# Tying the weight scans to a tile of their own, splitting an exchange in four, and starting running sums with a copy

## The chip, the cores and the metric

The kernel runs on one core of a Trainium2 chip. The metric is the device time in microseconds (us) of one execution. A core has a matrix engine (PE, with its weight loads as PEld), a vector engine (DVE), a scalar engine (ACT), a general engine (POOL) and a sequencer that issues most of the DMAs (SP). Each engine and SP work through a list of instructions in a fixed order; an instruction that has to wait for a semaphore holds up all that stands behind it in the same list.

## What is computed

A transformer block on 2048 tokens of width D = 576: a layer norm that is shifted and scaled by a conditioning vector, linear attention with 32 heads, a residual, a second such norm, and a feed-forward layer of width 4608 with SiLU. Cut to what matters:

```python
mod = (silu(c) @ w_mod)                      # 6 vectors: sa, ca, ga, sb, cb, gb
h = layernorm(x) * (1 + ca) + sa
x = x + ga * attention(h, wqkv, wo)          # phi(q), phi(k), kv = phi(k)^T v, normalised
h = layernorm(x) * (1 + cb) + sb
x = x + gb * (silu(h @ w1) @ w2)             # w1: 576 x 4608, w2: 4608 x 576
```

The kernel takes the feed-forward products in 16-bit halves (a rounded part and a rest). So that nothing overflows, the weights and values are scaled by powers of two, and these powers are found from the weights themselves: a sum of squares over the columns of w1 and over the rows of w2.

## The kernel before

The hidden width of 4608 is cut into 18 groups `g` of 256 columns. Two neighbouring groups share one set of scale factors (`factor`, lines 201 to 203). To find the factors of such a pair, `scans` (line 737) loads 512 columns of `B_w1` and 512 rows of `B_w2` piece by piece (line 759, on SP) and squares each piece on ACT with a running total (line 760). `find_factors` (line 763) then adds the totals on DVE (770, 771), writes them to DRAM (772) and reads them back to all partitions (773), which is the exchange of limits, and goes on with about ten tiny instructions: a reduce (774), a multiply (775), a maximum (776), a power on POOL (777), then a mask, reciprocals and products on DVE (778 to 787).

The work has three stages.

1. *Tiles.* A loop over 16 tiles `t` of 128 tokens projects keys and values (`k_proj`, `v_proj`; line 285 is the matmul), adds up `kv_mm` (712) and, for the first half, projects queries. The tokens of the next four tiles are loaded as a block (`load_block`, 333), normalised, turned by way of DRAM (`turn_block`, 340 to 350) and modulated (`turn`, 255 and 261) on the way. PE follows the order of the text. The order of the other engines is written out by hand in `FIRST` and laid on by `arrange`, as no-wait dependencies from each instruction to the one before it in the list.
2. *Attention output and the first group.* A loop over steps `s`: `q_norm`, `q_transpose`, `attn_out`, the second norm, and the feed-forward of group 0. In its end, and in the first two slots of the third stage, group 1 is worked with products of a Strassen kind, and their order is written out in `ORDERS`.
3. *Groups 2 to 17.* 32 slots, in an order found when the kernel is built by a planner (`Schedule`) with a duration for every step and named rooms that are read and written. Running sums are kept in `accb` and in four rooms `U`, which POOL sets to zero (1791) before `down_add` (1661) adds the first product from PSUM.

The scans and factor arithmetic of the first pair (groups 0 and 1) belong to stage 1, in `find_first`, called at the end of each tile; those of the second pair (groups 2 and 3) belong to stage 2, in `find_second`, called at the start of each step; the later pairs are steps of the planner. The instructions of the first two are `loose`: they are in no hand-written order, and the scheduler puts each where its simulation finds the engine free and the operands there. So a scan may stand in ACT's list a long way ahead of the tile in whose text it is.

Of the kernel before, what the change touches and what calls it, by code (L numbers as in the profile page):

```python
# [24 lines left out]
def kernel(ctx: ExitStack, tc, A_x, A_wqkv, A_wo, B_x, B_w1, B_w2, c, w_mod, out):  # L25
# [117 lines left out]

    def loose(*made):
        free.update(i.ins.name for i in made)

    def arrange(orders, start):
        for engine, text in orders.items():
            traced = [i for i in nc.cur_bb.bb.instructions[start:] if i.engine == getattr(mybir.EngineType, engine)
                      and i.name not in free  # L150
                      and not isinstance(i, (mybir.BassTilePoolBoundary, mybir.InstTileManualSchedule, mybir.InstRegisterMove))]
            before = None
            for part in text.split():
                first, *last = part.split("-")
                for i in traced[int(first) : int(last[0] if last else first) + 1]:
                    if before is not None:
                        no_wait = mybir.DependencyInfo(mybir.DependencyClass.NoSync, mybir.DependencyReason.DATA)
                        tc.add_manual_dep(i, before.name, no_wait, reason="arrange")
                    before = i
# [39 lines left out]
    sets = [const.tile([P, 8], F32, name=f"set{i}") for i in range(2)]  # L199

    def factor(g, name):
        i = ("beta", None, "delta", "gamma", "inv", "kappa", "out", "ratio").index(name)
        return sets[g // 2 % 2][:, i : i + 1]
# [533 lines left out]
    def scans(G_, spots, st, n, width):  # L737

        f0 = 2 * G_ * FW
        made = []  # L740
        for j in range(0, 9, n):
            m = min(n, 9 - j)
            spot = spots[len(made) % len(spots)]
            at_, to = spot[:, : m * FW], st[:, 0, j // n : j // n + 1]
            load = [(at_[64 * h : 64 * h + 64], B_w1[:, f0 + h * FW : f0 + (h + 1) * FW].rearrange("(p j) f -> p j f", j=9)[:, j : j + m])
                    for h in range(2)]
            made.append((load, at_, to, m))
        flat = B_w2[f0 : f0 + 2 * FW, :].rearrange("a b -> (a b)").rearrange("(p n) -> p n", p=P)
        k = 0
        while k < 4 * D:  # L750
            m = min(width, 4 * D - k)
            spot = spots[len(made) % len(spots)]
            to = st[:, 1, k // width : k // width + 1]
# [3 lines left out]
        for load, at_, to, m in made:  # L757
            def fetch_part(load=load, m=m):
                return [nc.sync.dma_start(dst if m is None else dst.rearrange("p (j f) -> p j f", j=m), src) for dst, src in load]
            parts.append((fetch_part, lambda at_=at_, to=to: A.activation(at_, at_, AF.Square, accum_out=to)))  # L760
        return parts

    def find_factors(G_, st, n1, n2, small, every):

        own, q, half = small[:, 0:2], small[:, 2:6], small[:, 6:10]
        s8, before = sets[G_ % 2], sets[(G_ + 1) % 2]
# [47 lines left out]
    first_scans = scans(0, [z], found, 2, D)  # L814
    first_steps = [step for _, step in find_factors(0, found, 5, 4, crowp[:, 12:22], z[:, : 2 * P])]

    def scan_first(n):
        if 0 < n <= len(first_scans):
            loose(first_scans[n - 1][1]())
        if n < len(first_scans):  # L820
            loose(*first_scans[n][0]())

    def find_first(t):

        if t == 2:
            loose(V.memset(crowp[:, 18:22], 0.5))
# [21 lines left out]
    if True:  # L848
        for t in range(NT):
            tb, i = t // 4, t % 4  # L850
            more = tb + 1 < NB
            if i == 0 and more and t > 0:
# [46 lines left out]
            find_first(t)  # L899
# [4 lines left out]
    with tc.manual_schedule(engines={mybir.EngineType.PE}):  # L904
# [64 lines left out]
        for j in range(KC + 1):  # L969
# [12 lines left out]
            if j in (0,):  # L982
                q_proj(next(qs))
    psA.release()
# [279 lines left out]
    slots = [(1, 0), (1, 1)] + [(g, p) for i in range(2, NG, 2) for p in range(2) for g in (i, i + 1)]  # L1264
# [153 lines left out]
    def find_second(s):  # L1418

        if s == 8:  # L1420
            rest = rests["hT"][0]
            spots = [rest[:, 1152 * i : 1152 * i + 1152] for i in range(2)]
# [688 lines left out]
```

## Time and profile before

| | us |
|---|---|
| median of 3 runs | 1131.14 |
| the runs | 1127.79 to 1132.87 |
| the profiled execution | 1126.87 |
| its span (first to last instruction) | 1125.2 |
| PE busy | 1083.8 |
| DVE busy | 899.4 |
| ACT busy | 690.5 |
| POOL busy | 655.8 |

The page gives busy time for each engine; a waits answer says what ended the idle time in front of an instruction; a timeline answer lists an engine's instructions in order of time, with the idle time ahead of each in square brackets and the name of what released it. A windows answer gives the busy time of each engine in a stretch, then the TensorE clock that was granted (1.00 is full) and the load of the DMA engines. Since PE is busy for nearly all of the span, the places where it is not are what counts.

### The profile page before, as it was taken

The numbers are of one execution on the slowest core, as the hardware profiler recorded it, in microseconds if no ns is written. First come the engines' busy times: TensorE is split into PE (matmuls) and PEld (weight loads), VectorE is DVE, ScalarE is ACT, GpSimd is POOL, SyncE is SP. The second block draws the span as 40 slices with busy tenths as digits, with TensorE's granted clock in tenths as the row PEclk, the third lists the DMA queues.
The fourth block names the chain that finished last, engine by engine and source line by source line (L and its number), as shares of the span: only waits on it lengthen the run. The fifth ranks groups of instructions, "written<-read, shape, count | busy, mean of one in ns | idle before, by whom it ended". The sixth has DMA issues, their size and how long they took to land.

```text
span 1125.2 us, 19368 instructions
## 1 busy us (share of the span) xinstructions
PE 1083.8 (96%) x7137; PEld 777.7 (69%) x7137; DVE 899.4 (80%) x1478; ACT 690.5 (61%) x1336; POOL 655.8 (58%) x759
## 2 busy tenths in 40 slices
PE   8799999998999988899999999999999999999998
PEld 7788999898888544566666666666666666666665
DVE  7548865757797989989889889789889789888757
ACT  5633442354655668777677677677677677676654
POOL 3300000254472468958958948848948848957663
PEclk9999999999999999999999999999999999999999
DMA  9494958062224565858666656656567657635522
GB/s 287 123 226 83 163 144 108 9 171 58 77 95 149 202 219 174 284 128 264 200 187 225 207 178 225 203 181 226 199 183 227 202 181 226 209 114 178 172 84 106
DMA packets 120079, 193.53 MB, mean 172 GB/s; under 512 B 43372, under 2 KB 78064, under 8 KB 119984
## 3 DMA queue, kind: packets, MB, share of 16 engines
q1 hardware_dynamic: 119812, 191.99, 58.2%
q8 instruction: 56, 0.92, 0.3%
q14 instruction: 39, 0.32, 0.1%
q10 hardware_dynamic: 172, 0.30, 0.1%
HBM read 176.77 MB, written 15.48 MB: 171 GB/s over the span
## 4 chain that ended last, share of the span: by engine, by line
PE 78%; DMA 9%; DVE 5%; ACT 3%; POOL 2%; issue 1%; SPq 1%; ACTq 0%; DVEq 0%; POOLq 0%
PE up L1566 30%; PE down L1650 29%; PE psK L285 8%; PE big L285 5%; DMA z<-in_B_w_dram 3%; PE small L1080 2%; PE big L1091 1%; DMA acc<-in_A_wqkv_dram 1%; DMA hT<-in_B_w_dram 1%; DMA hT<-hd 1%; DMA xt<-in_A_x_dram 1%; PE kvp L712 1%; PE psK L975 1%; PE small L270 1%; PE big L1005 1%
## 5 line engine op out<-in xcount | busy, mean ns | idle before, releaser
L1566 PE MATMUL up<-hT,w 128*128 128x512 f16 x1264 | 317.9, 381 | 7.9 <-DMA hT<-hd 4.7
L1566 PEld LDWEIGHTS <-w 128*128 128x128 f16 x1492 | 146.5, 98 | 143.2 <-issue 10.6
L1659 DVE SCALAR_TENSOR_TENSOR acc<-acc,set,down 128x576 f32<-128x576 f32 x128 | 103.6, 810 | 31.2 <-PE down L1650 29.7
L1584 ACT ACTIVATE f<-f,set 128x512 f32<-128x512 f32 x102 | 73.4, 720 | 77.4 <-DVE f L1590 67.6
L285 PE MATMUL psK<-w,hT 128*128 128x256 f32 (+1 forms) x638 | 104.3, 300 | 10.4 <-DVE vx L162 5.8
L1604 POOL TENSOR_TENSOR s<-f,f 128x256 f32<-128x256 f32 x66 | 54.0, 818 | 100.9 <-ACT f L1585 98.5
L285 PEld LDWEIGHTS psK<-w,hT 128*128 128x128 f32 x638 | 92.7, 191 | 12.2 <-issue 6.1
L1650 PE MATMUL down<-w,hb 128*128 128x288 f16 x600 | 89.3, 287 | 3.4 <-DVE U L1661 3.4
L1650 PE MATMUL down<-w,hc 128*128 128x288 f16 x600 | 88.9, 286 | 0.0
L1650 PE MATMUL down<-w,hT 128*128 128x288 f16 x480 | 82.8, 286 | 0.4 <-DVE acc L1661 0.4
L1588 DVE TENSOR_TENSOR f<-up,p 128x512 f32<-128x512 f32 x102 | 69.7, 683 | 16.2 <-PE up L1566 10.6
L1650 PEld LDWEIGHTS <-hb 128*128 128x128 f16 x600 | 58.9, 98 | 25.5 <-issue 3.0
L1585 ACT ACTIVATE f<-f,set 128x512 f32<-128x512 f32 x102 | 73.6, 722 | 3.3
L1650 PEld LDWEIGHTS <-hc 128*128 128x128 f16 x600 | 58.7, 98 | 21.5
L238 POOL TENSOR_TENSOR rstd<-ve,neghalf 128x4 f32<-128x4 f32 (+3 forms) x10 | 9.9, 992 | 108.4 <-DVE ve L237 107.6
L1628 POOL TENSOR_TENSOR hc<-s,hc 128x512 f16<-128x512 f32 x50 | 62.7, 1254 | 5.0 <-ACT hc L1624 5.0
L1650 PEld LDWEIGHTS <-hT 128*128 128x128 f16 x480 | 47.0, 98 | 26.6 <-issue 0.8
L1590 DVE TENSOR_TENSOR f<-up,f 128x512 f32<-128x512 f32 x68 | 46.8, 688 | 19.3 <-PE up L1566 18.5
L1601 POOL TENSOR_TENSOR s<-f 128x256 f32<-128x256 f32 x66 | 55.9, 848 | 8.9 <-ACT f L1581 7.1
L285 PE MATMUL big<-w,qT 128*128 128x288 f32 x352 | 54.7, 304 | 4.0 <-DVE qT L162 3.9
L1608 POOL TENSOR_TENSOR f<-f,s 128x256 f32<-128x256 f32 x66 | 50.4, 763 | 12.8 <-DVE hb L1628 9.0
L1606 POOL TENSOR_TENSOR s<-s,f 128x256 f32<-128x256 f32 x66 | 54.8, 830 | 3.0
(378 smaller groups left out, 2698.7 us busy)
## 6 DMA issues: line engine op xcount, KB each, us to landing
hT<-hd SPq DMA_DIRECT2D x101, 640.0 KB, 4.4
hT<-hd SPq DMA_DIRECT2D x65, 512.0 KB, 4.1
hT<-in_B_w_dram SPq DMA_DIRECT2D x16, 576.0 KB, 6.8
hT<-in_B_w_dram SPq DMA_DIRECT2D x32, 256.0 KB, 4.6
raw<-in_B_w_dram SPq DMA_DIRECT2D x9, 576.0 KB, 4.0
v<-in_B_w_dram SPq DMA_DIRECT2D x9, 576.0 KB, 6.2
xt<-in_A_x_dram SPq DMA_DIRECT2D x16, 288.0 KB, 7.1
raw<-in_w_mod_dram SPq DMA_DIRECT2D x8, 576.0 KB, 6.8
```

What stands on the lines that cost most here:

```text
L285: T.matmul(ps, xpart(a), wpart(b), start=n == 0, stop=n == len(XW) - 1)
L1566: T.matmul(ps, left, right, start=first and m == 0, stop=m == len(seq) - 1, skip_group_check=True)
L1584: A.activation(f, f, AF.Silu, scale=factor(self.g, "inv"))
L1585: loose(A.activation(f, f, AF.Identity, scale=factor(self.g, "delta")))
L1588: V.tensor_add(f, self.bank[bank[1]], self.p1)
L1601: G.tensor_sub(self.s3, half(i, 0, 0), half(i, 0, 1))
L1604: G.tensor_add(self.s[:, 0:1], half(i, 0, 1), half(i, 1, 1))
L1606: G.tensor_sub(self.s[:, 1:2], self.s[:, 0:1], half(i, 0, 0))
L1608: G.tensor_sub(half(i, 1, 0), half(i, 1, 0), self.s[:, 1:2])
L1628: eng.tensor_sub(t[:, :, 1, :], src, t[:, :, 0, :])
L1650: T.matmul(ps[:, p, :HALF], left[:, u, p * P : (p + 1) * P], right[:, v], start=n in (1, 5, 7, 6) and j == 0, stop=j == len(passes) - 1, s ...
L1659: V.scalar_tensor_tensor(dst, dst, factor(self.g, "ratio"), ps[:, :, :HALF], op0=ALU.mult, op1=ALU.add)
```

## The change

- `loose` now ties each of its instructions, with a no-wait dependency, behind the last ordered instruction that was traced before it on its own engine. What `loose` did before is now `aside`, and is still used for the second activation of a value.
- `find_first` is called twice in each tile, at its start and at its end. The loads of piece `n` come at the end of tile `n + 2`, its square at the start of the next tile. The limits of the modulation vectors move by half a tile; the first part of the exchange stays at the end of tile 12, the second at the end of tile 13, the next four instructions come at the start of tile 15, and the rest after the products for the attention output (behind the loop that ends in line 983, called as tile 17).
- `find_second` follows a small table: loads at steps 6, 8 and 9, squares at 8, 9 and 10, and the exchange with its arithmetic in four parts at steps 11, 12, 13 and 14. The pieces land in the unused halves of two weight rooms, which are free earlier than the room used before, and the limits are read into the unused half of a third.
- There are three sets of factors instead of two, in the planner's rooms too.
- The rooms `U` are no longer set to zero; the first product of group 1 is copied into them. Four memsets of one column each keep POOL's numbering.
- The planner's beats for the down products are written as lists of 14; they are the same numbers as before. `GROUPS` holds the same pairs.

```diff
+    def follow(i, before):
+        no_wait = mybir.DependencyInfo(mybir.DependencyClass.NoSync, mybir.DependencyReason.DATA)
+        tc.add_manual_dep(i, before.name, no_wait, reason="arrange")
+
+    def aside(*made):
+        free.update(i.ins.name for i in made)
+
     def loose(*made):
-        free.update(i.ins.name for i in made)
+
+        aside(*made)
+        for i in made:
+            for before in reversed(nc.cur_bb.bb.instructions):
+                if before.engine == i.ins.engine and listed(before):
+                    follow(i.ins, before)
+                    break
...
-    sets = [const.tile([P, 8], F32, name=f"set{i}") for i in range(2)]
+    sets = [const.tile([P, 8], F32, name=f"set{i}") for i in range(3)]
+    GROUPS = [(g, g + 1) for g in range(0, NG, 2)]
...
-    def find_first(t):
-
-        if t == 2:
+    def find_first(t, late):
+
+        if t == 2 and late:
             loose(V.memset(crowp[:, 18:22], 0.5))
-        if 2 <= t <= 11:
-            scan_first(t - 2)
-        if t == 9:
+        n = t - 2
+        if late and 0 <= n < len(first_scans):
+            loose(*first_scans[n][0]())
+        if not late and 0 < n <= len(first_scans):
+            loose(first_scans[n - 1][1](found))
+        if t == 9 and late:
             load_limit(bc["gb"], sb)
-        if t == 10:
+        if t == 11 and not late:
             find_limit(1, bc["gb"])
-        if t == 11:
+        if t == 11 and late:
             load_limit(z, vec[0])
-        if t == 12:
+        if t == 12 and late:
             loose(*(step() for step in first_steps[0:3]))
+        if t == 13 and not late:
             find_limit(0, z)
             find_limit(2, bc["gb"])
-        if t == 13:
             find_bounds()
+        if t == 13 and late:
             loose(first_steps[3]())
-        if t == 15:
-            loose(*(step() for step in first_steps[4:]))
+        if t == 15 and not late:
+            loose(*(step() for step in first_steps[4:8]))
+        if t == 17:
+            loose(*(step() for step in first_steps[8:]))
...
+            small = rest[:, 2324 + 10 * k : 2334 + 10 * k]
+            if k not in second_steps:
+                second_steps[k] = [step for _, step in find_factors(k, st, *n, small, rests["wt"][0])]
+            if what[0] == "A":
+                loose(G.memset(small[:, 6:10], 0.5))
+            a, b = {"A": (0, 3), "B": (3, 4), "C": (4, 8), "D": (8, None)}[what[0]]
+            loose(*(step() for step in second_steps[k][a:b]))
+
+    SECOND = {6: "L10 L11", 8: "S10 S11 L12 L13", 9: "S12 S13 L14", 10: "S14", 11: "A1", 12: "B1", 13: "C1", 14: "D1"}
...
+            elif self.g == 1 and n == 1:
+                V.tensor_copy(dst, ps[:, :, :HALF])
             else:
                 V.tensor_add(dst, ps[:, :, :HALF], dst)
...
-        for u in U:
-            G.memset(u, 0.0)
+        for i in range(NB):
+            G.memset(small_room[:, 22 + i : 23 + i], 0.0)
...
-            plan.add(eng.replace("Pool", "POOL"), 0.12 if eng != "SP" else 0.1, step, [], ["stats", f"factors{G_ % 2}"] + wait, lag=7.0 if eng == "SP" else 0.0)
+            plan.add(eng.replace("Pool", "POOL"), 0.12 if eng != "SP" else 0.1, step, [], ["stats", f"factors{G_ % 3}"] + wait, lag=7.0 if eng == "SP" else 0.0)
```

Before, `find_second` loaded two pieces at a time at steps 8 to 10, squared them a step later, and had the exchange at steps 12, 13 and 15.

More of the change, by code (lines that the diff above doesn't have):

```diff
@@ L734, with scans @@
     qs = iter(range(NT))
-    def scans(G_, spots, st, n, width):
-        f0 = 2 * G_ * FW
+    def scans(G_, spots, width):
+        f0, cols = GROUPS[G_][0] * FW, len(GROUPS[G_]) * FW
+        half, n2 = cols // 2, cols * D // P
+        n = min(width, 4 * FW) // half
         made = []
@@ L983 @@
                 q_proj(next(qs))
+        find_first(17, False)
     psA.release()
@@ L1532, in __init__ @@
             self.f, self.a, self.ps, self.t, self.bank = {}, {}, {}, {}, {}
+            self.other = g > 1 and pair == 1 and g == GROUPS[set_of[g]][0]
         def step(self, token):
@@ L1614, in room @@
         def room(self, name, i, n):
-            if self.g % 2 == 0 and self.pair and f"{name}{i}" in others:
+            if self.other and f"{name}{i}" in others:
                 return others[f"{name}{i}"]
@@ L1877, in room_name @@
         room = f"{name.replace('hp', 'hc')}{i}"
-        return f"{room}.{2 if u.g % 2 == 0 and u.pair and room in others else u.g % 2}"
+        return f"{room}.{2 if u.other and room in others else u.g % 2}"
     def token(u, t):
@@ L1889, in token @@
             dst = {1: f"U{b}", 6: f"U{b}", 7: f"c{b}11", 5: f"c{b}11", 2: f"c{b}00", 4: f"c{b}10", 3: f"c{b}01"}[n]
-            what = ("DVE", 0.82 if u.fresh and n not in (5, 6) else 0.77, [bank[u, "ps", m], f"factors{u.g // 2 % 2}"], [dst])
+            what = ("DVE", 0.82 if u.fresh and n not in (5, 6) else 0.77, [bank[u, "ps", m], f"factors{set_of[u.g] % 3}"], [dst])
         elif name[0] == "f":
@@ L1894, in token @@
             if op == "~":
-                what = ("ACT", 1.5, [bank[u, "a"]] * ((i, k) == (0, 0)) + [f"factors{u.g // 2 % 2}"], [f])
+                what = ("ACT", 1.5, [bank[u, "a"]] * ((i, k) == (0, 0)) + [f"factors{set_of[u.g] % 3}"], [f])
             else:
```

130 lines of the change are left out of this document (66 added, 64 removed).

## The prediction

> **What bounds the kernel.** I read the page's busy times first, then busy time by stretches, then what PE waits for in the stretches where it is not busy.
>
> ```profile
> span 1125.2 us, 19368 instructions
> PE 1083.8 (96%) x7137; PEld 777.7 (69%) x7137; DVE 899.4 (80%) x1478; ACT 690.5 (61%) x1336; POOL 655.8 (58%) x759
> ```
>
> PE is busy for 1083.8 of 1125.2 us: all that a change of order can win is the other 41.4 us, and what a lower clock costs. The stretches show where these lie (columns: length, then busy time and count of each engine, granted clock, DMA load, GB/s).
>
> ```profile
> core 0: us, PE busy (x) PEld busy (x) DVE busy (x) ACT busy (x) POOL busy (x), PEclk, DMA share, GB/s
> ...
> 30.00:98.00 68.00, 57.13 (x402) 54.47 (x401) 40.19 (x90) 34.01 (x76) 9.91 (x7) 0.97 0.55 139
> 98.00:160.00 62.00, 62.00 (x472) 62.00 (x472) 47.79 (x79) 26.95 (x51) 1.29 (x1) 1.00 0.91 169
> 160.00:210.00 50.00, 46.67 (x354) 46.27 (x353) 32.23 (x70) 12.92 (x30) 3.35 (x6) 1.00 0.57 75
> 210.00:235.00 25.00, 24.63 (x152) 21.87 (x151) 14.13 (x27) 9.73 (x18) 8.99 (x9) 1.00 0.17 51
> 235.00:271.00 36.00, 31.03 (x224) 30.37 (x223) 23.62 (x59) 15.40 (x26) 18.89 (x21) 0.95 0.51 127
> 271.00:386.00 115.00, 112.32 (x802) 91.94 (x801) 97.48 (x163) 72.89 (x120) 53.92 (x50) 1.00 0.35 119
> 386.00:480.00 94.00, 82.66 (x462) 45.94 (x460) 82.76 (x124) 66.36 (x132) 75.88 (x92) 0.96 0.68 225
> 480.00:1060.00 580.00, 580.00 (x3692) 361.01 (x3690) 496.44 (x756) 403.84 (x805) 439.87 (x528) 1.00 0.63 197
> ```
>
> In the planner's stage, 480 to 1060, PE never stops. It stands still for 68.00 - 57.13 = 10.9 us in 30:98, 3.3 in 160:210, 5.0 in 235:271, 2.7 in 271:386 and 11.3 in 386:480. The change touches all five places, so I look at what ends the waits in each.
>
> **Scans of the first pair, 30:98.** The nine squares stand in ACT's list at 31.7 to 84.5 us, in front of work that PE needs, and ACT waits at every one for its load (waits: total, times, longest).
>
> ```profile
> ACT z L760 <- DMA z<-in_B_w_dram: 18.6, 9, 3.4
> ...
> L760 ACT ACTIVATE z<-z x9: 421/634/686, 31.7 to 84.5; 128x512 f32<-128x512 f32 x4, 128x576 f32<-128x576 f32 x4, 128x256 f32<-128x256 f32 x1
> L760 ACT ACTIVATION_READ_ACCUMULATOR z<-z x9: 184/186/188, 32.2 to 85.1; 128x1 f32 x9
> ```
>
> ```profile
> PE psK L285 <- DVE vx L162: 3.6, 3, 2.2
> PE psK L285 <- DVE acc L420: 3.6, 3, 2.2
> PE psK L285 <- ACT hT L261: 1.5, 1, 1.5
> PE psT L285 <- DVE w L407: 0.7, 1, 0.7
> ```
>
> ```profile
> 65.66 0.68 ACT L760 ACTIVATE z<-z 128x576 f32<-128x576 f32 x1 [2.85 <-DMA z<-in_B_w_dram]
> 84.51 0.68 ACT L760 ACTIVATE z<-z 128x576 f32<-128x576 f32 x1 [3.44 <-DMA z<-in_B_w_dram]
> ...
> 67.81 0.49 PE L285 MATMUL psK<-w,hT 128*128 128x288 f32 x2 [2.19 <-DVE vx L162]
> 85.85 0.53 PE L285 MATMUL psK<-v,hT 128*128 128x288 f32 x2 [1.48 <-ACT hT L261]
> ```
>
> At 65.66 ACT has idled 2.85 us for a piece of weights; what stands behind it, the rounding of `vx`, lets DVE go on late, and PE starts its next pass 2.19 us late. At 84.51 it is the same with the modulated `hT`: 1.48 us. The chain of waits has that load as its longest transfer:
>
> ```profile
> 73.89 10.60 DMA z<-in_B_w_dram
> ```
>
> Of the 10.9 us idle, 0.7 (the wait for `w`) stands behind no scan. So at most 10.2 us can go; at least the two waits shown, 2.19 + 1.48 = 3.7, must. The other waits on `vx` and `acc` in this list come behind ACT waits of the same kind, so I am near the upper end and take 8.5; the rest I leave to what is late next, the first block's way through DRAM and back, which still has to be walked before tile 4. The clock adds to it:
>
> ```profile
> 68.00:73.00 5.00, 5.00 (x28) 5.00 (x28) 1.50 (x2) 0.00 (x0) 0.00 (x0) 0.66 1.07 218
> ...
> 120.00:150.00 30.00, 30.00 (x229) 30.00 (x228) 23.39 (x46) 12.04 (x24) 1.29 (x1) 1.00 1.04 155
> ...
> 266.00:271.00 5.00, 5.00 (x28) 5.00 (x28) 4.76 (x15) 0.00 (x0) 3.15 (x3) 0.66 0.15 51
> 403.00:407.00 4.00, 3.52 (x12) 1.68 (x12) 3.66 (x6) 3.02 (x6) 3.39 (x5) 0.58 0.10 34
> ```
>
> After the 2.19 us gap the clock was 0.66 over 68:73, which is 5.00 x 0.34 = 1.7 us lost. With the gap gone I take the 1.7 as won (bounds 0 and 1.7).
>
> What the squares cost in their new place, tiles 3 to 11: nine times 0.634 + 0.186 (the read of the total) is 7.4 us of ACT, which in 98:160 is busy 26.95 of 62 us. ACT's idle 35 us covers them. A load is issued once the square before it is done and has a tile until its own. A tile with a query pass is 94 matmuls (three passes of 28 and ten of `kv_mm`), so 98:160 with 472 is five tiles of 12.4 us; the slowest load took 10.60. On SP the nine loads now stand behind the block's loads and not ahead of them, with as many DMAs as before, so nothing of the block waits behind them. But 120:150 has a DMA load of 1.04, and tiles from 8 on, without a query pass, are shorter: 66 matmuls, which at 46.67 us for 354 is 8.7 us. Some of those squares may wait again. If one costs PE what it does now, 10.2 / 9 = 1.1 us, four cost 4.5; if none does, 0. I take 1.5.
>
> **Limits of the modulation, 160:210.**
>
> ```profile
> 164.11 0.75 DVE L796 TENSOR_REDUCE crow<-bc_gb 128x1 f32<-128x576 f32 x1 [2.31 <-DMA bc_gb<-vec]
> ...
> 201.97 0.42 DVE L774 TENSOR_REDUCE crow<-z 128x2 f32<-128x256 f32 x1 [1.04 <-DMA z<-limits]
> ...
> 166.07 0.51 PE L285 MATMUL psK<-w,hT 128*128 128x256 f32 x2 [1.45 <-DVE vx L162]
> ...
> 202.86 0.51 PE L285 MATMUL psK<-w,hT 128*128 128x256 f32 x2 [1.88 <-DVE vx L162]
> ```
>
> The reduce at 164.11 waits 2.31 us for a row of DRAM and stands in front of the last rounding of its tile, for which PE waits 1.45 us. In the changed text it comes at the start of tile 11, behind that rounding: -1.45 (bounds 0 and -1.45). The reduce of the exchanged limits at 201.97 moves behind its tile's last rounding in the same way, and its wait of 1.04 is taken off the 1.88 of PE: -1.0. The two waits before it on DVE, for the vectors themselves, stay. Sum: -2.5; with the 1.5 above, -1.0. The last part of the arithmetic, some eleven short instructions, none above the 0.42 of the reduce shown, and a product of 576 columns, at most the 0.75 of the other reduce, moves to about 232 us: under 5.4 us on DVE, which is busy 14.13 of 25 in 210:235 and so hides it. I cost it at nothing; without that cover it would be up to 5.4 us.
>
> **Second pair and the exchange, 235:271.**
>
> ```profile
> 260.56 0.42 DVE L774 TENSOR_REDUCE hT<-hT 128x2 f32<-128x256 f32 x1 [3.34 <-DMA hT<-limits]
> ...
> 263.59 1.13 DVE L778 TENSOR_SCALAR hT<-hT 128x4 int32<-128x4 int32 x1 [1.14 <-POOL hT L777]
> ...
> 264.92 0.81 DVE L162 TENSOR_TENSOR qT<-big,qT 128x640 fp32r<-128x640 f32 x1
> ...
> 265.79 4.12 PE L285 MATMUL big<-w,qT 128*128 128x288 f32 x20 [3.91 <-DVE qT L162]
> ...
> L760 ACT ACTIVATE hT<-hT x5: 420/1064/1171, 240.4 to 251.8; 128x1024 f32<-128x1024 f32 x2, 128x1152 f32<-128x1152 f32 x2, 128x256 f32<-128x256 f32 x1
> ```
>
> DVE stops 3.34 us for the limits to come back from DRAM, then 1.14 for POOL's power, and the rounding of `qT` is behind both; PE waits 3.91 us, and the clock is again 0.66 in 266:271, another 1.7 us. Moved to steps 11 to 14 in four parts, a tile lies between each transfer or power and its reader. The most that can go is 5.0 + 1.7 = 6.7; the least, if the wait for POOL stays and only that for the limits goes, 3.91 - 1.14 = 2.8. What is late next is DVE itself, 23.62 of 36 us busy here and 97.48 of 115 after. I take -5.
>
> In the new place the five squares are 2 x 1.06 + 2 x 1.17 + 0.42 and five reads of 0.186, 5.8 us, on ACT (72.89 of 115 busy in 271:386), and the arithmetic, fourteen instructions of at most 0.42, is under 5.9 us on DVE, which has 17.5 us to spare there while PE has 2.7. POOL's power (53.92 of 115 busy) moves behind the products of step 13; its reader is a step later. The loads at steps 6, 8 and 9 and the exchange at 11 and 12 stand on SP behind the loads of `x`, and those wait:
>
> ```profile
> SPq L956 <- POOL pn L953: 25.8, 5, 9.5
> ```
>
> So a part of the exchange may come later than its tile, and DVE would stop at the reader, with all `qT` behind it. Bounds: 0, and one such wait in full, 9.5 us. I take +1.5, nearer to the lower end, since a step lies between. Nobody needs the second pair's factors before the planner's stage, so their lateness itself costs nothing.
>
> **Rooms of the sums, 386:480.**
>
> ```profile
> 401.55 1.09 POOL L1791 MEMSET U<- 128x576 f32 x2
> ...
> 402.67 0.76 DVE L1661 TENSOR_TENSOR U<-down,U 128x576 f32<-128x576 f32 x1 [1.65 <-POOL U L1791]
> ...
> 403.48 1.50 PE L1650 MATMUL down<-w,hb 128*128 128x288 f16 x6 [3.42 <-DVE U L1661]
> ```
>
> POOL sets two rooms to zero at 401.55, behind work of its own; DVE's first sum waits 1.65 us for it, the next sum frees the bank, and PE waits 3.42 us. Without the memsets DVE starts at 401.02, and PE's wait becomes 3.42 - 1.65 = 1.8 us: -1.65. The clock was 0.58 over 403:407, 1.7 us lost; whether a gap of 1.8 still does that is open (bounds 0 and -1.7), I take half, -0.85. Four memsets, two of them 1.09 us, leave POOL (75.88 of 94 busy): a gain between 0 and 2.2. POOL has 18 us to spare there, so 0. A copy out of PSUM has no row; it takes the place of four sums of 0.76, so it wins between 0 and 3.0 us of DVE's 82.76 and loses nothing unless it is slower than a sum with one operand more. I take 0, the sum being its nearest row.
>
> [...]
>
> **Three sets, new room names.** The planner no longer makes a set wait for the readers of the set two pairs back. PE is busy for 580.00 of 580 there, so there is nothing to win: 0. DVE's 83.6 us of idle time (580 - 496.44) hide a changed order; if they did not, see the second rival.
>
> **Sum:** -8.5 - 1.7 - 1.0 - 5.0 + 1.5 - 1.65 - 0.85 + 0 = -17.2 us, on the profiled execution (1126.87, span 1125.2) 1109.7. That execution lies 4.3 us under the median of the three runs, 1131.14; for the median I take the same difference: 1114.
>
> **Rivals.** 0.5% of the time, 5.7 us, is about what a measurement can tell here; the three runs spread over 5.1.
>
> *The waits move with the scans.* ACT still arrives before its loads, in tiles where PE has nothing idle to give. For it: ACT waited at all nine, 2.1 us each, and the DMA load of 1.04. Against: a tile of 8.7 to 12.4 us, and the slowest of the loads took 10.60. Then the 8.5 and the 1.0 come back, the 1.7 of clock with them, and the exchange gives 3 of its 5: -17.2 + 8.5 + 1.0 + 1.7 + 2 = -4, that is 1127. It decides from about 1.1 us of PE for each scan.
>
> *The planner's order gets worse*, the slower one. The room names are part of what it sorts by, and one stage of 580 us with no idle time has only that to lose. At 0.54 us for each of the 32 slots the gain is gone, at 0.72 the kernel is slower by 0.5%; I put it at 0.75: +24, that is 1138. Against: with fewer conflicts the planner has no less choice, and no engine but PE is above 86% there.
>
> *The exchange is late on SP.* One wait of the row above at full length, 9.5 us, stops DVE and reaches PE in place of my 1.5: -17.2 + 8.0 = -9.2, 1122. For it: the waits on SP. Against: the exchange has a step to itself.
>
> **How the numbers follow.** Forecast 0.55; late exchange 0.20; waits that move 0.13; planner 0.12. Faster by over 0.5%: 0.55 + 0.20 = 0.75; within: 0.13; slower: 0.12. The likeliest is 1114. All upper bounds together, -10.2 - 1.7 - 2.5 - 6.7 - 1.65 - 1.7 - 2.2 = -26.7, give 1104, the low end; the high end takes in the waits that move and no change at all, 1131, and leaves out the planner's case.
>
> **What would show it.** Squares of `z` between about 60 and 170 us, one to a tile, with ACT waits for them near 0 and not 18.6; PE in 30:98 idle by under 3 us and no low clock near 68. No wait of PE for `qT` of more than 1 us near 260, none of the vector engine for limits. DVE's reduce of the second exchange in 310:350, with PE idle in the second stage no more than 2.7 + 1.5. No memset in front of the first `U`. 580 us from the first planned slot on with PE full. The prediction is wrong if ACT's waits for scans stay above 10 us, if PE has idle time in the planner's stage, or if the block's way through DRAM holds tile 4 where it was.

## The result, and the profile after

The changed kernel takes 1127.12 us (median of 20 runs, 1122.54 to 1131.39), the kernel before 1131.04 (20 runs, 1127.48 to 1133.14). The ratio is 0.9971, with a 95% interval of 0.9958 to 0.9984: by it the change wins 3.3 us. That is clear of zero, but inside the half per cent (5.7 us) that the prediction took as the least that can be told. 17 us were forecast. The profiled execution of after took 1127.2 us, with a span of 1125.5; that of before, 1126.87 and 1125.2.

The same total hides large movements. First the page, and busy time by stretches of after (same columns as before):

```profile
span 1125.5 us, 19357 instructions
PE 1083.3 (96%) x7137; PEld 778.4 (69%) x7137; DVE 899.7 (80%) x1478; ACT 692.8 (62%) x1336; POOL 662.5 (59%) x759
```

```profile
30.00:98.00 68.00, 62.84 (x467) 61.59 (x467) 48.44 (x97) 32.72 (x68) 10.21 (x7) 1.00 0.53 134
98.00:160.00 62.00, 54.59 (x392) 54.18 (x391) 37.58 (x66) 24.20 (x48) 1.29 (x1) 0.94 0.82 154
160.00:210.00 50.00, 46.12 (x338) 45.76 (x338) 28.31 (x47) 17.56 (x40) 2.34 (x5) 0.97 0.67 103
235.00:271.00 36.00, 36.00 (x265) 35.04 (x264) 29.93 (x62) 12.94 (x20) 20.69 (x20) 1.00 0.39 111
386.00:480.00 94.00, 82.46 (x468) 45.99 (x466) 84.03 (x126) 66.19 (x132) 73.28 (x92) 0.98 0.69 228
480.00:1060.00 580.00, 580.00 (x3692) 360.98 (x3691) 493.57 (x756) 406.34 (x804) 448.78 (x527) 1.00 0.64 197
```

In 30:98 PE issued 467 matmuls where it had issued 402, at full clock: the gain forecast there came, though 5.2 us of idle time are left where under 3 were expected. In 235:271 it never stops, as forecast. But 98:160, which was full (62.00 of 62, 472 matmuls), has 54.59 us and 392 matmuls now, at a clock of 0.94.

A stretch cut at fixed times mixes gain and shift. PE runs the same 7137 matmuls in the same order in every kernel here, so I count from one matmul to another by its number. I begin at the 184th, since the code ahead of it is the same everywhere and its start varies between executions (31.2 to 35.9 us).

| us from matmul to matmul | before | after | difference |
|---|---|---|---|
| 184 to 574 (head, scans of before) | 65.82 | 56.95 | -8.87 |
| 574 to 1454 (rest of the first stage) | 120.56 | 135.06 | **+14.50** |
| 1454 to 1841 (second pair, exchange) | 62.53 | 55.38 | -7.15 |
| 1841 to 2638 | 122.89 | 122.20 | -0.69 |
| 2638 to 2884 (behind the first `U`) | 52.38 | 53.15 | +0.77 |
| 2884 to 7042 (planner's stage) | 654.01 | 654.19 | +0.18 |
| sum | 1078.19 | 1076.93 | -1.26 |

The table is of one execution each. That of before lies 4.2 us under its median and that of after on it, so the sum falls short of the 3.3 us of the ratio. Kernels below that share the code of a stretch show how far single executions differ: 64.27 to 65.82 us from 184 to 574 and 119.86 to 120.56 from 574 to 1454 (before, E1, E7, E8), 62.53 to 65.25 from 1454 to 1841 (before, E2, E7). Part of this can be the clock, 0.94 in 235:271 in E7 and 0.95 before; the last section has more on it. The +14.50 is far outside.

One stretch of six eats the gain. There PE waits for one thing, three times (PE's waits, 98 to 215 us):

```profile
PE psK L302 <- DVE vx L177: 11.3, 3, 4.7
```

and ACT, between 30 and 215 us, waits for the loads of the scans longer than before (18.6 us then):

```profile
ACT z L780 <- DMA z<-in_B_w_dram: 26.8, 7, 5.8
```

One of the three places, with all engines shown (start, length, engine, line; in brackets the idle time before and what ended it):

```profile
116.78 0.63 ACT L780 ACTIVATE z<-z 128x512 f32<-128x512 f32 x1 [5.69 <-DMA z<-in_B_w_dram]
...
117.40 0.35 ACT L715 CAST vx<-psK 128x252 fp32r<-128x252 f32 x1
...
117.79 0.42 DVE L177 TENSOR_TENSOR vx<-psK,vx 128x252 fp32r<-128x252 f32 x1 [7.33 <-ACT vx L715]
...
119.99 0.81 PE L302 MATMUL psK<-w,hT 128*128 128x288 f32 x2 [4.72 <-DVE vx L177]
```

This is the chain of before (square, rounding of `vx` on ACT, its remainder on DVE, the next pass on PE), only longer. The transfers themselves aren't slow. The trace's answer for the tile `z` gives the issues, and the time from issue to landing, which the trace has for four of these 14 issues:

```profile
L779 SPq DMA_DIRECT2D z<-in_B_w_dram x14: 361/599/652, 64.6 to 197.3; - x14
...
DMA to landing us min/median/max: 3.2/5.0/7.6
```

The slowest load of before took 10.60. So the loads are issued late: six of the seven waits are for loads that went out 4 to 26 us after their tile was free. The other (5.47 us, before the square at 82.36) is for a load that went right behind its square, at 74.06, and took 7.6 us to land. SP's own timeline shows why the six are late, around the square at 116.78 and the next (its tile was free again at 91.5, after the square at 90.79):

```profile
108.70 0.58 SPq L667 DMA_DIRECT2D parts<-tmod  x1
110.20 1.84 SPq L779 DMA_DIRECT2D z<-in_B_w_dram  x2
116.08 0.39 SPq L673 DMA_DIRECT2D raw<-parts  x1
116.52 10.85 SPq L373 DMA_DIRECT2D raw<-in_w_mod_dram  x2
127.47 1.13 SPq L779 DMA_DIRECT2D z<-in_B_w_dram  x2
```

The load for the square at 116.78 was free to go at 91.5 and went at 110.20, behind the next block's way through DRAM and directly behind a store of the modulation's partial sums. The next was free to go at 117.5 and went at 127.47, behind two rows of modulation weights, of which the second was held until about 127. These transfers wait for work on DVE (SP's waits, 60 to 215 us):

```profile
SPq L742 <- DVE vx L177: 9.3, 1, 9.3
...
SPq L373 <- DVE tmod L663: 6.7, 1, 6.7
...
SPq L667 <- DVE tmod L665: 6.0, 1, 6.0
```

Further on it is the same with the output weights, which wait for `vx`:

```profile
175.09 10.98 SPq L742 DMA_DIRECT2D raw<-in_A_wo_dram  x3
186.17 0.36 SPq L779 DMA_DIRECT2D z<-in_B_w_dram  x1
```

So one delay feeds the next: SP waits for DVE, DVE waits for ACT's `vx`, ACT waits for a load, and the load stands on SP behind the transfer that waits for DVE. In the kernel before, all nine loads stand on SP ahead of the first store of partial sums, because nothing tied them to the written order. The last of them and that store, in before:

```profile
73.89 0.36 SPq L759 DMA_DIRECT2D z<-in_B_w_dram  x1
...
116.86 0.58 SPq L650 DMA_DIRECT2D parts<-tmod  x1
```

They paid for it in the head, where the waits were 18.6 us. The change put six of the nine behind that store.

### The profile page after: what moved, and what is told of

Read it like the earlier page. It is cut to its first block, busy times and chain, and to the rows that moved or that the text cites. A ratio compares the mean times of both kernels' runs of the same rounds, so it can differ in the third digit from the quotient of the medians.

```text
span 1125.5 us, 19357 instructions
## 1 busy us (share of the span) xinstructions
PE 1083.3 (96%) x7137; PEld 778.4 (69%) x7137; DVE 899.7 (80%) x1478; ACT 692.8 (62%) x1336; POOL 662.5 (59%) x759
## 4 chain that ended last, share of the span: by engine, by line
PE 75%; DMA 8%; DVE 6%; POOL 4%; ACT 4%; issue 1%; SPq 1%; POOLq 0%; ACTq 0%; DVEq 0%
PE up L1595 29%; PE down L1679 28%; PE big L302 7%; PE psK L302 4%; DMA z<-in_B_w_dram 2%; DMA acc<-in_A_wqkv_dram 2%; PE small L1103 1%; DMA xt<-in_A_x_dram 1%; PE big L1114 1%; DMA turned<-acc 1%; PE psK L997 1%; PE big L1028 1%; PE small L287 1%; DVE st L249 1%; PE kvp L729 1%
## 5 line engine op out<-in xcount | busy, mean ns | idle before, releaser
L302 PE MATMUL psK<-w,hT 128*128 128x256 f32 (+1 forms) x638 | 106.8, 305 | 14.2 <-DVE vx L177 13.1
L302 PEld LDWEIGHTS psK<-w,hT 128*128 128x128 f32 x638 | 95.4, 197 | 15.4 <-issue 14.0
L1637 POOL TENSOR_TENSOR f<-f,s 128x256 f32<-128x256 f32 x66 | 53.0, 803 | 17.1 <-DVE hb L1657 9.4
L1679 PE MATMUL down<-w,hd 128*128 128x288 f16 x396 | 55.1, 288 | 0.0
```

The source lines that it names most:

```text
L302: T.matmul(ps, xpart(a), wpart(b), start=n == 0, stop=n == len(XW) - 1)
L1637: G.tensor_sub(half(i, 1, 0), half(i, 1, 0), self.s[:, 1:2])
L1679: T.matmul(ps[:, p, :HALF], left[:, u, p * P : (p + 1) * P], right[:, v], start=n in (1, 5, 7, 6) and j == 0, stop=j == len(passes) - 1, s ...
```

## The experiments

Each kernel is given by its difference. Ratios are to the kernel before, run beside it on the same chip, with 95% intervals; times are medians. Times between matmuls are from each kernel's profiled execution.

**E1, the first pair as before.** In the first stage the ties are off and the calls stand in one place again.

```diff
+    tied, loose = loose, aside
-            find_first(t, False)
             ...
-            find_first(t, True)
+            find_first(t)          # the kernel before's function
-        find_first(17, False)
+        loose = tied
```

> The changed kernel, with the scans, limits and scale arithmetic of the first pair put back where the kernel before had them (in one place at the end of each tile, in no written order). The second pair, the rooms U and the three sets stay as changed. Theory 1 (the first pair's loads, now tied into SP's list, wait there behind transfers that wait themselves, and this costs about 14.5 us between 98 and 215 us, more than the 8.9 us that the tie saved between 30 and 98): the idle time between 30 and 98 comes back (PE again at about 54 of 68 us), matmul 1454 starts near 218 us again instead of 225.4, the gain of the second pair (about 7 us by matmul 1841) is kept, and the time is about 5 to 8 us below the kernel before: 1123 to 1126. Rival A (the loss between 98 and 215 comes from elsewhere in the change, such as the three sets or the rooms): matmul 1454 stays near 225 us and the time is above the kernel before, about 1136. Rival B (the second pair's gain was only time made up that the first pair had lost): matmul 1841 starts near 280 us as in both, and the time is that of before, 1131.

Measured: 1121.18 us, ratio 0.9923 (0.9904 to 0.9941), 8.7 us under before, a little more than the 5 to 8 expected. Head 65.20, then 119.87, then 55.37: the three stretches are those of before, before and after.

```profile
98.00:160.00 62.00, 62.00 (x473) 62.00 (x472) 47.58 (x80) 26.86 (x52) 1.29 (x1) 1.00 0.86 167
...
235.00:271.00 36.00, 36.00 (x278) 36.00 (x277) 29.09 (x56) 16.26 (x27) 22.24 (x23) 1.00 0.33 96
```

The loss in 98:160 belongs to the first pair's part, and the rest of the change is worth 8.7 us. Rivals A and B fall.

**E2, the first pair alone.** The kernel before, with only the new `find_first` and the ties for it.

```diff
+    loose = tie                    # for the first stage only
-        if 2 <= t <= 11: scan_first(t - 2)
+        ...                        # the changed find_first(t, late)
+        find_first(17, False)
+        loose = aside
```

> The kernel before with only the first pair's part of the change (scans, limits and scale arithmetic tied and placed as in the changed kernel). Theory 1: matmul 574 starts near 90 us instead of 97.5, matmul 1454 near 225 instead of 218, and the time is 5 to 8 us above the kernel before: 1136 to 1139. Rival A (the loss comes from elsewhere in the change): matmul 1454 starts near 211 and the time is 7 to 9 us below before, near 1123. Rival B (what the first pair loses is made up later whatever the second pair does): the time of before.

Measured: 1133.09 us, ratio 1.0031 (1.0015 to 1.0046), 3.5 us above before. Head 57.51 (-8.3 against before), then 132.16 (+11.6). PE's waits from 98 to 215 us, 11.3 in after, are here:

```profile
PE psK L304 <- DVE vx L181: 8.9, 3, 3.7
```

The sign and the places are as theory 1 has them, the size is smaller than the 5 to 8 us expected: I had taken the whole 14.5 from one execution of after, and this kernel loses 11.6. The first pair's part as made is a loss.

**E3, the loads from ACT's queue.** Whether it is SP's list or the transfers.

```diff
-        if late and 0 <= n < len(first_scans):
-            loose(*first_scans[n][0]())
+        if t == 2 and late:
+            loose(*first_scans[0][0](nc.scalar))
         if not late and 0 < n <= len(first_scans):
             loose(first_scans[n - 1][1](found))
+            if n < len(first_scans):
+                loose(*first_scans[n][0](nc.scalar))
```

> The changed kernel; the nine loads of the first pair's scans are issued from ScalarE's own queue instead of SP's, each right behind the square that frees the tile. Nothing else is changed. Theory 1 (the loads are issued late, because of what stands ahead of them in SP's list): ScalarE's waits for these loads between 60 and 215 us fall from 26.8 us to under 6, the waits of PE for vx at 120, 137 and 198 us (4.72, 2.69, 3.88) go, matmul 1454 starts near 212 us, and the time is 8 to 14 us below the changed kernel: 1113 to 1119. Rival C (the transfers themselves are slow among the block's other traffic, whichever queue issues them): the waits stay above 15 us and the time within 3 us of the changed kernel. Rival D (each square on ScalarE at its place in the order costs PE about as much as the wait: 1.1 us and more each): the waits for loads fall but matmul 1454 starts above 218 us, and the time is 1122 to 1126.

Measured: 1115.86 us, ratio 0.9877 (0.9857 to 0.9897): 13.9 us under before, and by the two ratios 10.6 under after. The stretch from 574 to 1454 takes 120.16, where after has 135.06. ACT's waits for these loads, 30 to 215 us, and the longer of the two that are left:

```profile
ACT z L780 <- DMA z<-in_B_w_dram: 7.3, 2, 5.9
```

```profile
79.60 0.63 ACT L780 ACTIVATE z<-z 128x512 f32<-128x512 f32 x1 [5.87 <-DMA z<-in_B_w_dram]
```

```profile
81.70 0.85 PE L302 MATMUL psK<-w,hT 128*128 128x256 f32 x2 [5.24 <-DVE acc L437]
```

Theory 1 holds, rival C (slow transfers) and rival D (the price of a square itself) fall. 7.3 is a little above the 6 expected: the first load, issued at 69.86 among other loads, takes 8.5 us, and its square is 5.87 us early. Issuing the loads from ACT saved 14.9 us between two matmuls (135.06 - 120.16), more than the issues themselves: the 14 issues of the nine loads on SP take some 8 us in all in after (median 0.599). What was saved as well is the time behind someone else's wait.

**E4, no scans in the first pair.**

```diff
-        if late and 0 <= n < len(first_scans): loose(*first_scans[n][0]())
-        if not late and 0 < n <= len(first_scans): loose(first_scans[n - 1][1](found))
+        if t == 3 and not late: loose(V.memset(found, 1.0))
```

> The changed kernel without the nine loads and nine squares of the first pair: their sums are set to 1 by one instruction, so the limits of the first pair's weights are left out of the computation. This bounds what the scans cost where they stand. Theory 1: matmul 1454 starts at 208 to 212 us, and the time is 10 to 17 us below the changed kernel, close to the run with the loads on ScalarE's queue (within 4 us of it). Rival D (the squares' own time is the cost): more than 6 us below the run with the loads on ScalarE's queue. Rival A (the loss between 98 and 215 is not the scans'): within 4 us of the changed kernel.

Measured: 1107.01 us, ratio 0.979 (0.9765 to 0.9814). Head 53.63, then 117.60. That is 20.4 us under after by the ratios, more than the 10 to 17 expected, and 9.8 under E3, which by my own threshold of 6 spoke for the squares' price. E9 and E10 test that.

**E5, the first load early as well.** E3 with the first load at the end of tile 0.

```diff
-        if t == 2 and late:
+        if t == 0 and late:
             loose(*first_scans[0][0](nc.scalar))
```

> The run with the loads on ScalarE's queue, with one thing more: the first of the nine loads is issued at the end of tile 0 instead of tile 2 (its tile z has no earlier use). In that run the first load took 8.5 us to land, its square waited 5.87 us and PE stood 5.24 us behind it, with 3.4 us of lower clock after. Theory 1, continued (a square must find its load landed; nothing else there costs much): this wait goes, the clock is full between 30 and 98 us, the second square's wait of 1.48 us stays, and the time is 5 to 7 us below that run: 1109 to 1111. Rival E (PE is held there by something else of the block as well, so that the gap stays under another name): less than 2 us gained, 1114 to 1116.

Measured: 1113.35 us, ratio 0.9854 (0.9834 to 0.9875). Head 57.51 (E3: 61.66), then 120.30. The wait of 5.24 is gone, but between the ratios lie 2.6 us and not 5 to 7, so neither reading of the expectation is met; the granted clock in 30:98 is 0.97, where E3 has 0.95, and it is low from 89.77 on (0.66 in 89:94), behind the wait shown in the last section.

**E6, on SP but untied.** The same queue as in after, another place in it.

```diff
         if not late and 0 < n <= len(first_scans):
             loose(first_scans[n - 1][1](found))
+            if n < len(first_scans):
+                aside(*first_scans[n][0]())     # SP, not tied
```

> The changed kernel; the loads of the first pair's scans stay on SP but are no longer tied to SP's list: each is written right behind the square that frees its tile and put where the builder's own order places it, which is ahead of the row of partial sums, ahead of the gather of the sums and ahead of the output weights. The squares stay tied on ScalarE. Theory 1 (only the place among SP's waiting transfers matters, not the queue): ScalarE's waits for the loads between 60 and 215 us fall from 26.8 us to under 8 and the time is within 4 us of the run with the first load early on ScalarE's queue: 1108 to 1114. Rival F (a load that waits for its square now holds the block's stores and loads behind it on SP; three loads stand in a row ahead of the second block's turning): PE waits appear between 85 and 130 us and the time is 1118 to 1126.

Measured: 1114.03 us, ratio 0.9864 (0.9841 to 0.9886). Head 55.82, then 122.49. SP's timeline:

```profile
73.70 18.68 SPq L779 DMA_DIRECT2D z<-in_B_w_dram  x6
...
108.66 1.81 SPq L779 DMA_DIRECT2D z<-in_B_w_dram  x2
111.49 0.58 SPq L667 DMA_DIRECT2D parts<-tmod  x1
```

The fourth load, which after issues at 110.20, is in the last two of the six issues that end at 92.4 (73.70 + 18.68); the fifth goes at 108.66 and not at 127.47, ahead of the partial sums. The last one is out by 151, ahead of the output weights. ACT still waits for loads (30 to 215 us), and PE hardly notices (98 to 215 us):

```profile
ACT z L780 <- DMA z<-in_B_w_dram: 14.4, 4, 4.6
```

```profile
PE psK L302 <- DVE vx L177: 1.2, 1, 1.2
PE psK L302 <- DVE a L437: 1.1, 1, 1.1
```

So it was the place in SP's list and not the queue. The 8 us that I expected for ACT's waits was too low; the time came out at the edge of the expected 1108 to 1114. Rival F (the block held by loads that wait) falls: PE's longest wait between 85 and 130 is 1.85, and after has nearly the same one (1.84).

**E7, the rooms U alone**, and **E8, the second pair and the three sets alone**.

```diff
 # E7: the kernel before, with
-        for u in U:
-            G.memset(u, 0.0)
+        for i in range(NB):
+            G.memset(small_room[:, 22 + i : 23 + i], 0.0)
+            elif self.g == 1 and n == 1:
+                V.tensor_copy(dst, ps[:, :, :HALF])
 # E8: E1, with these lines the other way round
```

> The kernel before with only the rooms U begun by a copy instead of a memset and an add. The prediction gave this 2.5 us (1.65 us of wait and 0.85 us of clock near 403). Theory G (the wait at U falls as predicted, but the engines behind it, with their 2.99 us of wait at 440 us and the loads, take it back before the planned stage): PE's wait at U near 1.7 us, no low clock at 404, and a time within 1 us of the kernel before. Rival H (what is gained stays): 2 to 3 us below the kernel before.

> The kernel before with only the second pair's part and the three sets: scans and scale arithmetic of the second pair tied, the exchange of its limits in four parts; the first pair as before, the rooms U by memset as before. Theory 1: the stretch 235 to 271 us has PE busy all of its 36 us at full clock (before 31.03, 0.95), and the time is 5 to 8 us below before. With theory G for the rooms it is within 1 us of the run that also had the copy into U (8.7 us below before); with rival H it is 2 to 3 us above that run. Rival B (the second pair only makes up what the first had lost): less than 2 us below before.

Measured: E7 1128.92 us, ratio 0.999 (0.9973 to 1.0007); E8 1124.04, ratio 0.9948 (0.9929 to 0.9968). PE's wait at the first `U` in E7 (in E8, with the memset, it is 3.4 us as in before):

```profile
PE down L1650 <- DVE U L1661: 1.7, 1, 1.7
```

The wait halves as forecast. What that is worth in the end: 1.1 us by E7 against before, 2.8 us by E1 against E8 (0.9923 against 0.9948). Both are compatible with 2.5 and with half of it; between theory G and rival H these runs can't decide. E8 gives the second pair 5.9 us, and PE is full in 235:271 with the first pair as before, so it isn't making up someone else's loss.

**E9, squares without loads, and E10, loads without squares.** E5 split in two.

```diff
 # E9
-            loose(*first_scans[0][0](nc.scalar))
+            loose(G.memset(z, 1.0))
-            if n < len(first_scans):
-                loose(*first_scans[n][0](nc.scalar))
 # E10
+        if t == 2 and late:
+            loose(V.memset(found, 1.0))
-            loose(first_scans[n - 1][1](found))
```

> The run with the first load early on ScalarE's queue, without the nine loads: its nine squares read a tile that GpSimd has set to 1 once, so the limits of the first pair's weights are left out of the computation. This run and the next split the 6.3 us that still lie between that run (1113.35) and the one without scans (1107.01). Theory S (ScalarE's own 0.82 us for each square, 7.4 us in all, on a stage where PE waits for ScalarE and VectorE in turn): the time stays within 2 us of 1113. Theory L (the loads: their issue on ScalarE, the two waits of 4.2 and 4.3 us for them, their traffic beside the block's): 1106 to 1109.

> The run with the first load early on ScalarE's queue, without the nine squares: the loads are issued at the same places, their sums are set to 1 by one instruction, so the limits of the first pair's weights are left out of the computation. Theory S: near the run without scans, 1106 to 1109. Theory L: within 2 us of 1113.

Measured: E9 1106.59 us, ratio 0.9819 (0.9792 to 0.9846); E10 1111.27, ratio 0.9848 (0.9825 to 0.9870). From matmul 184 to 1454: no scans 171.23, squares alone 170.97, loads alone 175.93, both (E5) 177.81. By these counts the nine squares cost PE between nothing (170.97 against 171.23) and 1.9 us (177.81 against 175.93), the loads 4.7 to 6.8. The ratios give the squares 0.7 us (E5 against E10) to 3.3 (E9 against E4) and the loads 4.0 to 6.6, with intervals that overlap. So theory L holds in the main: E4's distance to E3 was mostly not the squares, and at under 0.4 us each they are far from the 1.1 of rival D. ACT's timeline of E10 shows one way in which the loads cost:

```profile
79.06 1.89 ACTq L779 DMA_DIRECT2D z<-in_B_w_dram  x2
81.00 0.65 ACT L432 ACTIVATE e<-psK 128x576 f32<-128x576 f32 x1 [5.91 <-DMA z<-in_B_w_dram]
```

The exponential at 81.00 needs no load, but stands in ACT's queue behind an issue that waits for the load before it to land. In E5 one exponential waits 4.3 us in this way, and one square 4.2 us for its own load.

**E11, the loads from GpSimd's queue.** E5 with `nc.gpsimd` for `nc.scalar`.

```diff
-                loose(*first_scans[n][0](nc.scalar))
+                loose(*first_scans[n][0](nc.gpsimd))
```

> The run with the first load early on ScalarE's queue, with all nine loads issued from GpSimd's queue instead. The loads were found to cost 5 to 6 us, the squares next to nothing. Theory L1 (the cost is ScalarE's: it issues the loads, and twice the work behind an issue or a square waited over 4 us there): PE's waits at 83.5 and 89.3 us go down, and the time is 3 to 6 us below that run: 1107 to 1110 at the pace of 1130 for before, a ratio of 0.980 to 0.983. Theory L2 (the cost is the loads' traffic beside the block's, whichever engine issues them): within 2 us of that run, a ratio of 0.984 to 0.987. Rival P (GpSimd issues such loads slowly, and they land late): above 1116, over 0.987.

Measured: 1111.22 us, ratio 0.9834 (0.9815 to 0.9853). Head 56.10, then 119.18. It is the fastest complete kernel here, 1.7% under before, but only 0.2% under E5, and the two intervals overlap. The ratio lies between the two expected bands (0.980 to 0.983 and 0.984 to 0.987): how much of the loads' 5 us is ACT's and how much is their traffic stays open. Of PE's two waits named ahead, the one of 1.31 us at 83.5 is gone; the other, 1.85 us, stays. That one, 1.83 to 1.85 us at matmul 574, is in after, E2, E5, E6, E10 and E11, whichever engine issues the loads, and not in E4 and E9, which have none, so this part doesn't belong to ACT's queue. On GpSimd's queue the 14 issues took 0.588 us each (median), and ACT waited for one load, 4.7 us; rival P falls.

## Why the prediction was wrong

**The step that failed** is the one on the squares' new place: "A load is issued once the square before it is done and has a tile until its own", and "On SP the nine loads now stand behind the block's loads and not ahead of them [...] so nothing of the block waits behind them". I asked who would wait behind the loads and not what the loads would wait behind. A load's tile is free about a whole tile ahead of its square, but SP went through its list in order: in after a load free at 91.5 us went at 110.20. The rows that would have told it were in the kernel before already, as waits of SP on DVE (60 to 215 us); I had used such a row for the second pair only:

```profile
SPq L650 <- DVE tmod L648: 8.2, 1, 8.2
...
SPq L725 <- DVE vx L162: 4.5, 1, 4.5
```

ACT's waits for scans came to 26.8 us, over the 10 that the prediction named as a sign of being wrong. The term was +1.5 us. In its place E2 against E4, which differ in the scans here, show 132.16 - 117.60 = 14.6 us, and after against E4 135.06 - 117.60 = 17.5. Of these, 11.3 are PE's waits for `vx` and 5.2 the clock (62 x 0.06 in 98:160, 50 x 0.03 in 160:210). With the loads on GpSimd's queue the same difference is 119.18 - 117.60 = 1.6, on ACT's 2.7, untied on SP 4.9. So from 574 on, 1.5 is near for squares whose loads come in time. From 184 on, with the head, the scans cost 4.0 (E11), 6.6 (E5) and 7.1 us (E6) against E4, so even then 1.5 was low.

**The rival "the waits move with the scans"** had the right number, 1127, and the right first half: ACT arrives before its loads. Its reason, slow transfers at a DMA load of 1.04, is not what happened: the four landings that the trace has took 3.2 to 7.6 us. The agreement of its number is luck: it gives back the whole gain of the head and 2 of the exchange's 5 us, while the head kept 8.9 and the exchange 7.15, and 14.5 were lost in another stretch. Its threshold of 1.1 us of PE for each scan was passed: 14.6 / 9 is 1.6.

**Head, -8.5, and clock near 68, -1.7.** Right in kind: no low clock there (1.00 in 30:98, before 0.97), and PE's idle time in 30:98 is 5.2 us in place of 10.9. Over matmuls 184 to 574 both together gave 8.9 us in after and 8.3 in E2, of 10.2. In E4, with no scans at all, they give 12.2.

**Limits of the modulation, -2.5.** Right as far as it can be read: with the scans out of the way (E4), 574 to 1454 is 117.60 against 120.56, which is 3.0 us; no scan of before stood in that stretch.

**Second pair and exchange, -5.0, its new place +1.5.** Undersized: 1454 to 1841 gives -7.15 in after and the same 55.4 us in every kernel that has this part. The forecast's upper bound was 6.7. The new place cost 1.1 of the 1.5 us. The stretch 1841 to 2638 hides it, 122.20 against 122.89, for it ends with the wait at `U`, which is 1.7 us shorter in after; with the rooms alike it is 123.96 (E8) against 122.89 (before), and 122.20 (E1) against 121.15 (E7). By these counts the two come to 6.1 us together, by E8's ratio to 5.9. The mechanism of the 1.1 was another than the forecast's: the feared late exchange didn't reach PE, and DVE doesn't wait for the limits there. What after has and before hasn't is a wait of PE of 0.83 us at 307.7 for ACT's rounding of `qT`, with a square on ACT at 303.20 ahead of it; that the square causes it is likely, not tested.

**Rooms U, -1.65 and -0.85.** The wait fell from 3.42 to 1.7 (forecast 1.8), and the clock near 403 is full (1.00 in 403:407, before 0.58). Behind it, 2638 to 2884, after takes 0.77 us more than before, although it has 1.7 us less of low clock there. PE's waits, 385 to 480 us, before and then after:

```profile
PE up L1566 <- DMA hT<-hd: 4.7, 3, 2.7
PE down L1650 <- DVE U L1661: 3.4, 1, 3.4
PE up L1566 <- DVE f L1588: 2.3, 2, 2.1
PE up L1566 <- ACT p L1541: 0.9, 1, 0.9
```

```profile
PE up L1595 <- DMA hT<-hd: 3.3, 2, 2.4
PE up L1595 <- DVE f L1617: 3.2, 2, 3.0
PE up L1595 <- ACT p L1570: 1.8, 1, 1.8
PE down L1679 <- DVE U L1690: 1.7, 1, 1.7
```

The three other waits are 7.9 us before and 8.3 after, and after has 1.6 us of new, shorter waits for DVE at `down`. So PE gives part of the gain back to the engines behind; why they aren't earlier wasn't tested. From matmul 1841 to 2884 the copy is worth 1.4 us (E7 against before) and 1.5 (E1 against E8), by the ratios 1.1 and 2.8, where 2.5 were forecast.

**Planner, 0.** Right: 580.00 of 580 in both, and 654.0 against 654.2 us from matmul 2884 on.

The parts add up: E2 +3.5, E8 -5.9, U between -1.1 and -2.8 make -3.5 to -5.2, and after measures -3.3. Where the loads are issued in time, the change is worth 15.4 (E6), 16.5 (E5) and 18.8 us (E11), against a forecast of 17.2. So the one term decides the miss. That the rest comes so near is in part luck, since errors cancel: of the 17.2, the first stage was to give 11.2, the second pair 3.5 with its new place and the rooms 2.5; E11 has 11.1 from 184 to 1454, the second pair gives 6.1 and the rooms some 1.5.

## What to carry to other kernels

A transfer that is tied into a queue's written order inherits every wait that stands ahead of it there: here a load that was free at 91.5 us went at 110.20. For a moved DMA, read both directions of its queue: who waits behind it, and what it now waits behind; the waits of the issuing queue in the kernel before give the second. When a move frees one stretch and the total stays, count from one instruction to the same instruction in both traces: one stretch will show the loss, and what waits there names the queue. Take a second execution before believing a difference of a microsecond or two.

## What the runs showed of the hardware

In these runs the clock doesn't follow from the length of a wait alone. Two kernels have the same wait of 1.84 us at the same matmul, after and then E5:

```profile
90.31 0.50 PE L302 MATMUL psK<-w,hT 128*128 128x288 f32 x2 [1.84 <-DVE vx L177]
```

```profile
89.29 0.51 PE L302 MATMUL psK<-w,hT 128*128 128x288 f32 x2 [1.84 <-DVE vx L177]
```

After keeps its clock (1.00 from 85.88 to 92.70); E5 has half of it for 3.41 us from 89.77 on (after first):

```profile
85.88:89.29 3.41, 2.59 (x20) 2.35 (x18) 3.17 (x9) 1.57 (x3) 1.37 (x1) 1.00 0.02 8
89.29:92.70 3.41, 2.39 (x18) 2.42 (x19) 3.41 (x7) 2.23 (x6) 0.00 (x0) 1.00 0.02 5
```

```profile
86.36:89.77 3.41, 1.57 (x12) 1.36 (x11) 3.27 (x9) 3.07 (x6) 0.11 (x1) 1.00 0.00 0
89.77:93.18 3.41, 3.41 (x17) 3.41 (x16) 3.38 (x7) 0.73 (x3) 0.00 (x0) 0.50 0.31 87
```

So behind the same wait the clock costs E5 1.7 us (half of 3.41) and after nothing. Of the six kernels with this wait, E2, E5, E10 and E11 have a clock of 0.97 in 30:98, after and E6 of 1.00.

After itself loses it at 137.08, behind a wait of 2.69 us (0.57 in 137:141). Before has a wait of 2.69 us as well, at 455.86, and keeps it there (1.00 in 450:480). I had left half of the 1.7 at `U` open; there, with 1.7 us of wait in after, the clock stayed full (1.00 in 403:407). What decides between the two wasn't shown.
